# One multiplication of the second attention unit moved from VectorE to GpSimd, and the first stage's pieces put in another order

## The chip, the cores and the metric

The kernel runs on one core of a Trainium2 chip. A core has five engines that work side by side, each through its own list of instructions in order: TensorE (PE in the profile; its weight loads are listed apart as PEld), VectorE (DVE), ScalarE (ACT), GpSimd (POOL) and SyncE (SP), which here only starts DMA transfers. They share the on-chip memory SBUF, and TensorE writes its products into PSUM, a small memory of banks from which VectorE and ScalarE read. An engine waits for another on semaphores. The metric is the device time of one execution in microseconds; a time below is the median of several runs.

## The reference: what is computed

Two blocks in a row, all in float32. The first is a linear recurrent attention (RWKV-6) over batch 4, 8 heads, 768 steps, head width 48; the second a token and channel mixer.

```python
for t in range(S):                                   # S = 768
    cur = einsum('bhd,bhe->bhde', u * k_t, v_t)      # the step's own product, weighted by u
    y_t = einsum('bhd,bhde->bhe', r_t, state + cur)
    state = w_t[..., None] * state + einsum('bhd,bhe->bhde', k_t, v_t)
x = y.transpose(0, 2, 1, 3).reshape(B, S, 384)
u = x + (relu(x.T @ w_tok1) @ w_tok2).T              # 768 -> 256 -> 768 over the tokens
out = u + relu(u @ w_ch1) @ w_ch2                    # 384 -> 1536 -> 384 over the channels
```

## The kernel before, in words

The attention is cut into chunks of 64 steps, so that most of it becomes matrix products. A *unit* is a third of a batch (256 steps, which is four chunks, and 8 heads in four pairs): units 0, 1 and 2 are batch 0, and there are twelve in all. For each unit the code makes a set of *pieces*, small functions with names, and a table or a planner decides in which order the pieces are issued. The pieces of a unit `i`, by the names of the table:

- `i.ends` (VectorE): running products of w from a chunk's end backwards (a scan, L446), and a reciprocal (L447). `i.begins` (VectorE): running products from the beginning (a scan in place over w, L454).
- `i.own0` to `i.own3` (ScalarE, L342): k times u, a pair of heads each, into one buffer that all units share. `i.own` (TensorE, L326): products of that with r. `i.put` (VectorE, L469): its diagonal into the attention matrix `at`.
- `i.keys` (VectorE, L451): k scaled in place by the products of `ends`. `i.queries` (VectorE, L457): r scaled in place by those of `begins`; it needs `begins`, the loaded r, and the end of `i.own`, which reads r unscaled.
- `i.tokens` (TensorE, L356): the scaled k turned, into two PSUM banks; `i.copied0`, `i.copied1` (ScalarE, L361) copy them out. `i.gram` (TensorE, L326): scaled k with scaled r; `i.mask` (VectorE, L338) picks its lower part into `at`.
- `i.carry` (TensorE, L376): each chunk's contribution to the state, in PSUM. `i.by0` to `i.by3` (ScalarE, L512) scale the state into SBUF and `i.up0` to `i.up3` (TensorE, L519) add it to the next chunk's: a chain in which ScalarE and TensorE take turns. `i.by0` of the next unit goes on from the last `up` of this one.
- `i.before` (TensorE, L391): r with the states; `i.seen` (ScalarE, L400) reads one column of it; `i.after` (TensorE, L412) adds `at` times v; `i.taken0` to `i.taken2` (ScalarE, L418) copy the result into x.

Beside these run the conversions of the mixer's weights, which come from DRAM as 64-bit words: `t0` to `t2` for the token weights and `c0` to `c2` for the first of the channel weights. Each has a `load` (a DMA), `plus` (L275) and `minus` (L278) on ScalarE, and `lead` (L281), `two` (L284), `value` (L288) and `sum` (L292) on VectorE. Then the first mixing of batch 0 begins: `h0` to `h11` (TensorE, L958) are x times the token weights, an even number for the first 128 hidden columns and an odd one for the second, one pair for each 128 tokens; `relu0` (ScalarE, L961) rectifies the even sum and `relu1` the odd one, and `back0` (TensorE, L969) multiplies with the second token weights, first the part of `relu0`, then that of `relu1`.

Everything of units 0, 1 and 2 and of `t`, all of `c0` but its `sum`, the loads of `c1` and `c2`, the `h`s and `back0` is the *first stage*. Its order is written out by hand as a table, `FIRST`. Each name is a piece; `a<b` is a DMA that may only be issued once piece `b` has been. `strict()` makes the instructions of TensorE, VectorE, ScalarE and SyncE follow each other on their engine in the order of the table; GpSimd is not in that list, so its instructions stand in the order in which the code made them and wait for their data alone. The rest of the kernel is issued from a second table, `ORDER`, of almost 1,200 characters that says from which of nine streams the next piece comes.

GpSimd sets up masks at the start and from 187 us on adds up a part of the hidden layer's forms (L776); in the first stage it has nothing to do after the masks.

Of the kernel before, what the change touches and what calls it, by code (L numbers as in the profile page):

```python
# [23 lines left out]
T = 64  # L24
# [24 lines left out]
LEAST, MOST = 2.0 ** -40, 2.0 ** 40  # L49
MID = 3 * G // 4 * SEG1  # L50
FIRST = (
# [8 lines left out]
)  # L60
ORDER = (
    "8880080880788088000008884844408008408040a80a88080880a484408848840a0a4480884080088880a80080884808884040488844488888084840"
# [13 lines left out]
def rwkv6_then_mixer(  # L76
# [16 lines left out]
    pe, dve, act, pool, sp = nc.tensor, nc.vector, nc.scalar, nc.gpsimd, nc.sync  # L93
# [92 lines left out]
    def w_of(i):  # L186
        return ws[i if i < UB else 1]
# [232 lines left out]
    def unit(i):  # L420
# [3 lines left out]
        w_, at = w_of(i), ats[i % 2 if i < UB else 0]  # L424
        by_chunk = [t[:ROWS].rearrange("p (g t) -> p g t", t=T) for t in (r_, k_)]
        L = {"before": {}}

        def of_chunks(t, first, n):
            return t[:ROWS, :G * SEG1].rearrange("p (g s) -> p g s", s=SEG1)[:, :, first:first + n]
# [24 lines left out]
            dve.tensor_tensor_scan(w_[:ROWS], w_[:ROWS], starts[:ROWS], 0.0, op0=ALU.mult, op1=ALU.add)  # L454

        def queries():
            dve.tensor_mul(by_chunk[0], by_chunk[0], of_chunks(w_, 0, T))  # L457

        def own_u(a):
            if a == 0:  # L460
# [83 lines left out]
        def each(f, n):  # L544
            return [lambda m=m: f(m) for m in range(n)]

        return dict(small=lambda: ranges(0), large=lambda: ranges(1), ends=ends, keys=keys, begins=begins, queries=queries, own_u=each(own_u, A),
                    own_gram=own_gram, copied=each(copied, UC), taken=each(taken, 3),
                    own_put=own_put, products=[lambda n=n: products(n) for n in range(3)], sums_put=sums_put,
# [804 lines left out]
```

## Time and profile before

| what | value |
|---|---|
| time, median of 3 runs | 477.82 us (477.06 to 478.12) |
| the profiled execution's own time | 476.31 us |
| its span, first to last instruction | 474.6 us |
| PE, DVE, ACT, POOL busy | 459.4, 344.8, 265.4, 54.1 us |
| granted TensorE clock, mean | 0.999 |
| end of the first stage (`back0` begins) | 48.79 us |

The profile's times are microseconds from the start of the span. A row of the timeline reads: start, duration, engine, line of the program, operation, written tile<-read tile with partitions x elements, how many instructions were merged, and in brackets the idle time of the engine ahead of it with what released it. A matrix product of float32 leaves two records in the trace, so 32 products show as x64. Line numbers of the trace are those of the kernel before; in the changed kernel each stands one line lower.

### The profile page before, as it was taken

The page shows a single profiled execution, that of the slowest core. Times are in us where ns is not written, and L with a number is a line of the kernel's source. Part 1 is how long each engine was busy: PE and PEld are TensorE (multiplying, and loading weights), DVE is VectorE, ACT ScalarE, POOL GpSimd, SP SyncE. Part 2 cuts the span into 40 slices and gives each one's busy share as a digit, 9 for nine tenths or more (in the row PEclk, how much of TensorE's full clock was granted, in tenths as well). Part 3 has the DMA queues.
Part 4 walks back from the last instruction along what each step waited for, and adds up shares of the span by engine and source line. Part 5 has one row for each costly group of instructions (what it writes and reads, how often), then busy time and mean ns, then how long its engine had stood idle before and what let it go on. Part 6 is the DMA issues. An engine that isn't in the chain of part 4 may idle for free.

```text
span 474.6 us, 12781 instructions
## 1 busy us (share of the span) xinstructions
PE 459.4 (97%) x5322; PEld 410.8 (87%) x5322; DVE 344.8 (73%) x495; ACT 265.4 (56%) x606; POOL 54.1 (11%) x58
## 2 busy tenths in 40 slices
PE   3999999999999999999999999999999999999996
PEld 2876688856797668999999999999999999999995
DVE  7988896779598877876897998685587885235341
ACT  5588788774678856353747485351827554034140
POOL 1000000000000001230303002130304003032130
PEclk9999999999999999999999999999999999999999
DMA  8955944573585456953888841754775612436231
GB/s 301 338 185 197 296 162 146 191 266 99 157 224 146 171 183 209 281 188 99 257 276 251 286 157 51 213 168 130 228 223 141 186 48 84 122 96 201 85 99 54
DMA packets 45055, 85.34 MB, mean 180 GB/s; under 512 B 4736, under 2 KB 37376, under 8 KB 44992
## 3 DMA queue, kind: packets, MB, share of 16 engines
q1 hardware_dynamic: 44704, 84.37, 56.1%
q8 instruction: 43, 0.70, 0.6%
q14 instruction: 20, 0.16, 0.1%
q10 hardware_dynamic: 288, 0.10, 0.1%
HBM read 72.65 MB, written 11.80 MB: 178 GB/s over the span
## 4 chain that ended last, share of the span: by engine, by line
PE 96%; DMA 1%; ACT 1%; SPq 0%; issue 0%; DVE 0%; DVEq 0%
PE bank L1015 10%; PE bank L783 8%; PE bank L790 8%; PE bank L785 8%; PE bank L801 8%; PE bank L803 8%; PE bank L802 8%; PE bank L1004 7%; PE bank L678 3%; PE bank L1000 3%; PE bank L737 3%; PE bank L326 2%; PE bank L391 2%; PE kv_ps L376 2%; PE bank L412 2%; PE h_ps L958 2%
## 5 line engine op out<-in xcount | busy, mean ns | idle before, releaser
L776 POOL TENSOR_TENSOR z_high<-z_high 128x384 fp32r<-128x384 f32 x48 | 52.9, 1106 | 405.0 <-DMA ring<-third 185.8
L765 ACT ACTIVATE z_high<-bank 128x384 fp32r<-128x384 f32 x48 | 23.5, 489 | 57.4 <-PE bank L790 56.9
L783 PE MATMUL bank<-x_forms,forms 128*128 128x384 f32 x216 | 50.3, 340 | 0.0
L790 PE MATMUL bank<-z_more,forms 128*128 128x384 f32 x216 | 50.1, 340 | 0.0
L785 PE MATMUL bank<-x_forms,ring 128*128 128x384 f32 x216 | 49.3, 337 | 0.0
L772 DVE SCALAR_TENSOR_TENSOR z_high<-bank,z_high 128x384 fp32r<-128x384 f32 x48 | 26.6, 555 | 31.4 <-ACT z_high L765 29.3
L1015 PE MATMUL bank<-wch,z 128*128 128x384 f32 x144 | 48.1, 488 | 0.0
L801 PE MATMUL bank<-forms,z_high 128*128 128x384 f32 x140 | 47.8, 342 | 0.0
L803 PE MATMUL bank<-forms,z_high 128*128 128x384 f32 x140 | 47.2, 337 | 0.0
L802 PE MATMUL bank<-ring,z_high 128*128 128x384 f32 x140 | 47.1, 337 | 0.0
L809 DVE SCALAR_TENSOR_TENSOR x<-bank,x 128x384 f32<-128x384 f32 x35 | 18.8, 553 | 38.9 <-PE bank L803 38.7
L1015 PEld LDWEIGHTS bank<-wch,z 128*128 128x128 f32 x144 | 26.8, 190 | 17.2
L512 ACT ACTIVATE before<-state,to_end 112x48 f32<-112x48 f32 x132 | 33.2, 324 | 13.0 <-DVE state L527 7.6
L790 PEld LDWEIGHTS bank<-z_more,forms 128*128 128x128 f32 x216 | 39.0, 188 | 0.1
L783 PEld LDWEIGHTS bank<-x_forms,forms 128*128 128x128 f32 x216 | 38.3, 188 | 0.5
L785 PEld LDWEIGHTS bank<-x_forms,ring 128*128 128x128 f32 x216 | 38.6, 188 | 0.0
L1004 PE MATMUL bank<-xT,wch 128*128 128x256 f32 x144 | 32.0, 381 | 0.0
L1004 PEld LDWEIGHTS bank<-xT,wch 128*128 128x128 f32 x144 | 27.0, 190 | 3.7
L768 ACT ACTIVATE z_high<-z_high 128x384 fp32r<-128x384 f32 x48 | 25.2, 525 | 3.6
L801 PEld LDWEIGHTS bank<-forms,z_high 128*128 128x128 f32 x140 | 26.3, 188 | 0.2
L802 PEld LDWEIGHTS bank<-ring,z_high 128*128 128x128 f32 x140 | 26.3, 188 | 0.0
L803 PEld LDWEIGHTS bank<-forms,z_high 128*128 128x128 f32 x140 | 26.3, 188 | 0.0
(250 smaller groups left out, 963.6 us busy)
## 6 DMA issues: line engine op xcount, KB each, us to landing
ring<-third SPq DMA_DIRECT2D x144, 192.0 KB, 3.3
raw<-in_words_ch_dram SPq DMA_DIRECT2D x8, 1023.8 KB, 4.9
rk<-in_rk_dram SPq DMA_DIRECT2D x36, 192.0 KB, 5.2
near<-in_near_dram SPq DMA_DIRECT2D x8, 768.0 KB, 4.9
w<-in_w_dram SPq DMA_DIRECT2D x10, 520.5 KB, 5.0
vt<-in_v_dram SPq DMA_DIRECT2D x12, 384.0 KB, 5.1
out_dram<-x SPq DMA_DIRECT2D x17, 192.0 KB, 2.1
third<-forms SPq DMA_DIRECT2D x12, 192.0 KB, 4.2
```

The lines of the kernel that those rows point to most:

```text
L512: act.mul(t[:ROWS, a], state[bt, g][:ROWS, a], by_last(c, j)[:, a:a + 1])
L768: act.mul(z_form(jt, 2), z_form(jt, 0).bitcast(f32), 1.0 / BASE)
L772: dve.scalar_tensor_tensor(z_form(jt, 1), a, 0.0, z_form(jt, 0).bitcast(f32), op0=ALU.max, op1=ALU.subtract)
L776: pool.tensor_add(z_form(jt, 2), z_form(jt, 2).bitcast(f32), z_form(jt, 1).bitcast(f32))
L783: pe.matmul(a, up[m], xf(0)[:, m], start=m == 0, stop=False)
L785: pe.matmul(a, low[:, m], xf(1)[:, m], start=False, stop=False)
L790: pe.matmul(banks["a", jt], joint, xf(2)[:, m], start=False, stop=m == 2)
L801: pe.matmul(a, z[0], up, start=first, stop=False, skip_group_check=True)
L802: pe.matmul(a, z[1], held[bt, s, half, 1, jt], start=False, stop=False, skip_group_check=True)
L803: pe.matmul(a, z[2], joint, start=False, stop=last, skip_group_check=True)
L1004: pe.matmul(ps, now["wch1"][:, jt // 4, m, ts(jt % 4, 128)], xT[:, m, ts(s, SEG)], start=(m == 0), stop=(m == DM // 128 - 1))
L1015: pe.matmul(ps, zs[s][:, jt, ts(n, 128)], now["wch2"][:, jt, :], start=(jt == 0), stop=(jt == NJ - 1))
```

## The change

`queries` of unit 1 is issued on GpSimd in place of VectorE; the operation and its operands are the same. And the table `FIRST` is replaced by another order of the same pieces: no piece is added or left out. Of the table's lines the last ones are shown.

```diff
 FIRST = (
...
-    "2.taken1 t2.value 2.taken2 h7 h8 c0.plus h10 t2.sum c0.minus c2.load<1.tokens c0.lead c0.two relu0 h9 h11 relu1 rk3 c0.value back0 "
+    "h7 h6 h9 h11 c1.load<2.own w3<2.by3 rk3 c0.minus h8 t2.value t2.sum c0.plus h10 relu1 c0.lead c2.load<1.tokens c0.two relu0 c0.value "
+    "back0 v3"
 )
...
         def queries():
-            dve.tensor_mul(by_chunk[0], by_chunk[0], of_chunks(w_, 0, T))
+            (pool if i == 1 else dve).tensor_mul(by_chunk[0], by_chunk[0], of_chunks(w_, 0, T))
```

Three places show what moves. VectorE first, in the stretch around the scaled r of unit 1. The tiles: `rk_89` is r and k of unit 1, `w_90` its w, `x` holds the w of unit 2 for now, and `first` on the left of a product is k of unit 2 or the second `at`. Before:

```order
L469 TENSOR_TENSOR first<-gram,u_rows 128x1024
L338 COPY_PREDICATED at_92<-before_it,gram 128x1024
L442 MEMSET starts 112x17
L446 SCALAR_TENSOR_TENSOR ahead<-x,starts 112x1041
L447 RECIPROCAL starts<-ahead 112x16
L457 TENSOR_TENSOR rk_89<-rk_89,w_90 112x1024
L451 TENSOR_TENSOR first<-first,ahead 112x1024
L281 TENSOR_TENSOR raw<-raw 128x1024
```

and in the changed kernel:

```order
L455 SCALAR_TENSOR_TENSOR w_90<-w_90,starts 112x1041
L339 COPY_PREDICATED at_92<-before_it,gram 128x1024
L443 MEMSET starts 112x17
L447 SCALAR_TENSOR_TENSOR ahead<-x,starts 112x1041
L448 RECIPROCAL starts<-ahead 112x16
L455 SCALAR_TENSOR_TENSOR x<-x,starts 112x1041
L470 TENSOR_TENSOR first<-gram,u_rows 128x1024
L452 TENSOR_TENSOR first<-first,ahead 112x1024
L282 TENSOR_TENSOR raw<-raw 128x1024
```

`1.queries` is gone from VectorE, `2.begins` (the scan over `x`) has come forward to stand right behind `2.ends`, and `1.put` stands behind both scans.

The second place is ScalarE between the end of unit 0 and the chain `by`/`up` of unit 1 (`before<-kv_ps,ahead` is a `by`). Before:

```order
L512 ACTIVATE before<-kv_ps,ahead 112x48 x4
L418 COPY x<-y_ps 128x8x48
L278 ACTIVATE raw<-raw,rebias 128x1024
L418 COPY x<-y_ps 64x8x48
L512 ACTIVATE before<-kv_ps,ahead 112x48 x4
L418 COPY x<-y_ps 64x8x48
L512 ACTIVATE before<-kv_ps,ahead 112x48 x4
```

and in the changed kernel:

```order
L513 ACTIVATE before<-kv_ps,ahead 112x48 x4
L343 ACTIVATE near<-first,u_col 112x2x128 x2
L419 COPY x<-y_ps 128x8x48
L343 ACTIVATE near<-first,u_col 112x2x128
L419 COPY x<-y_ps 64x8x48
L343 ACTIVATE near<-first,u_col 112x2x128
L513 ACTIVATE before<-kv_ps,ahead 112x48 x4
L279 ACTIVATE raw<-raw,rebias 128x1024
L513 ACTIVATE before<-kv_ps,ahead 112x48 x4
```

Between `1.by0` and `1.by1` the conversion step of 1,024 columns has given way to the four steps of `2.own`; a conversion step now stands between `1.by1` and `1.by2`.

The third is TensorE from `1.gram` on. Its list is the same up to there, piece by piece. Before:

```order
L326 MATMUL gram<-rk_89 64x64 x32
L519 MATMUL kv_ps<-before,ident 112x192
L391 MATMUL y_ps<-before,rk_89 64x48 x32
L376 MATMUL kv_ps<-vt,kT 48x48 x24
L519 MATMUL kv_ps<-before,ident 112x192
L958 MATMUL h_ps<-x,wtok_125 128x384 x2
L519 MATMUL kv_ps<-before,ident 112x192
L958 MATMUL h_ps<-x,wtok_125 128x384
L412 MATMUL y_ps<-vt,first 64x48 x32
```

and in the changed kernel:

```order
L327 MATMUL gram<-rk_89 64x64 x32
L392 MATMUL y_ps<-before,rk_89 64x48 x32
L520 MATMUL kv_ps<-before,ident 112x192
L959 MATMUL h_ps<-x,wtok_125 128x384 x2
L377 MATMUL kv_ps<-vt,kT 48x48 x24
L520 MATMUL kv_ps<-before,ident 112x192
L413 MATMUL y_ps<-vt,first 64x48 x32
L520 MATMUL kv_ps<-before,ident 112x192
L959 MATMUL h_ps<-x,wtok_125 128x384 x2
```

The `h`s stand in two pairs where there were a pair and single ones; seven `h`s end the stage in both kernels, even ones first before (`h8 h10`, then `h9 h11`) and odd ones first now (`h9 h11`, then `h8 h10`).

On SyncE's queue the load of unit 1's w stands two transfers earlier, `c1.load` stands ahead of the loads for unit 3, and the load of unit 3's v comes last.

14 rows, old and new, of the table FIRST are left out of this document.

## The prediction

> **What bounds the kernel now.** I read first the page's list of busy times, then the table by stage, then the timeline of the first 50 us, where everything lies that the change touches.
>
> ```profile
> span 474.6 us, 12781 instructions
> PE 459.4 (97%) x5322; PEld 410.8 (87%) x5322; DVE 344.8 (73%) x495; ACT 265.4 (56%) x606; POOL 54.1 (11%) x58
> ```
> ```profile
> 140.00:300.00 160.00, 159.72 (x1978) 143.15 (x1978) 131.19 (x192) 96.46 (x226) 22.59 (x20) 1.00 0.63 195
> ...
> 25.90:44.17 18.27, 17.52 (x601) 13.46 (x596) 15.23 (x17) 15.58 (x43) 0.00 (x0) 1.00 0.52 173
> 44.17:50.45 6.28, 6.28 (x26) 3.60 (x20) 5.31 (x7) 5.62 (x8) 0.00 (x0) 1.00 1.02 401
> ```
>
> Columns: stretch, length, then busy time of PE, PEld, DVE, ACT, POOL. TensorE sets the time. Between 140 and 300 us it stands still for 0.28 us of 160, so what the first stage saves or loses is passed on to the end almost whole. And the first stage itself is held by TensorE: from 25.9 us to the run of `h`s it is idle for 18.27 - 17.52 = 0.75 us, and from there to the end of `back0` for nothing. A new order of the same pieces can therefore win 0.75 us there and what single products waste, and no more.
>
> Where those 0.75 us lie, from the timeline of TensorE and ScalarE:
>
> ```profile
> 25.90 1.21 PE L376 MATMUL kv_ps<-vt,kT 64*48 64x48 f32 x64
> 27.04 0.58 PE L519 MATMUL kv_ps<-before,ident 112*112 112x192 f32 x2
> 27.55 1.16 PE L326 MATMUL gram<-first,near 48*64 48x64 f32 x64
> 29.23 0.58 PE L519 MATMUL kv_ps<-before,ident 112*112 112x192 f32 x2 [0.52 <-ACT before L512]
> ...
> 30.77 0.58 PE L519 MATMUL kv_ps<-before,ident 112*112 112x192 f32 x2 [0.20 <-ACT before L512]
> ...
> 40.23 0.91 PE L958 MATMUL h_ps<-x,wtok 128*128 128x384 f32 x2
> ...
> 44.17 4.78 PE L958 MATMUL h_ps<-x,wtok 128*128 128x384 f32 x14
> ```
> ```profile
> 26.19 0.48 ACT L418 COPY x<-y_ps 128x384 f32<-128x384 f32 x1 [1.03 <-PE y_ps L412]
> 26.56 1.22 ACT L278 ACTIVATE raw<-raw,rebias 128x1024 int16<-128x1024 int16 x1
> 27.81 0.48 ACT L418 COPY x<-y_ps 64x384 f32<-64x384 f32 x1
> 28.30 0.88 ACT L512 ACTIVATE before<-kv_ps,ahead 112x48 f32<-112x48 f32 x4
> ```
>
> `1.up1` at 29.23 and `1.up2` at 30.77 wait for ScalarE, 0.52 and 0.20 us, not for VectorE. `1.by1` could have begun when `1.up0` ended, at 27.62; it began at 28.30 since the conversion step of 1.22 us stood ahead of it. No wait of TensorE here is on the multiplication that moves.
>
> **The multiplication on GpSimd.** What it removes and what stands in its place:
>
> ```profile
> 10.32 1.23 DVE L457 TENSOR_TENSOR rk<-rk,first 112x1024 f32<-112x1024 f32 x1 [0.24 <-PE gram L326]
> ...
> 15.46 2.31 DVE L454 TENSOR_TENSOR_SCAN w<-w,starts 112x1041 f32<-112x1041 f32 x1
> ...
> 17.69 1.20 DVE L451 TENSOR_TENSOR rk<-rk,ahead 112x1024 f32<-112x1024 f32 x1
> ...
> 19.11 1.22 DVE L469 TENSOR_TENSOR first<-gram,u_rows 128x1024 f32<-128x1024 f32 x1 [0.22 <-PE gram L326]
> ...
> 20.25 1.30 DVE L338 COPY_PREDICATED at<-before_it,gram 128x1024 f32<-128x1024 uint8 x1
> ...
> 21.61 2.33 DVE L446 TENSOR_TENSOR_SCAN ahead<-x,starts 112x1041 f32<-112x1041 f32 x1
> 23.98 0.26 DVE L447 RECIPROCAL starts<-ahead 112x16 f32<-112x16 f32 x1
> 24.15 1.16 DVE L457 TENSOR_TENSOR rk<-rk,w 112x1024 f32<-112x1024 f32 x1
> ...
> 27.82 0.69 DVE L281 TENSOR_TENSOR raw<-raw 128x1024 int16<-128x1024 int16 x1 [1.38 <-ACT raw L278]
> ...
> 31.27 1.23 DVE L292 TENSOR_TENSOR wtok<-wtok,raw 128x1024 f32<-128x1024 f32 x1
> ```
> ```profile
> 17.05 1.99 PE L326 MATMUL gram<-rk,near 48*64 48x64 f32 x64
> ```
> ```profile
> 187.72 1.02 POOL L776 TENSOR_TENSOR z_high<-z_high 128x384 fp32r<-128x384 f32 x1 [185.75 <-DMA ring<-third]
> ```
>
> VectorE loses one instruction of 1.16 us. GpSimd has done no product of 1,024 columns in this trace. Its addition of 384 columns takes 1.02 us alone; by width that is 1.02 x 1024/384 = 2.72 us, the upper bound for it undisturbed. If a part of it does not grow with the width, it is less: VectorE's 0.94 us for 768 columns (212.89, below) and 1.16 for 1,024 leave 0.28 us that are fixed, and with as much fixed on GpSimd it is 0.28 + 0.74 x 1024/384 = 2.25 us, the lower bound. I take 2.7, the nearer row being GpSimd's own. It can begin when `1.begins` and `1.own` are done. The list of TensorE up to `1.own` is unchanged, which puts that end at 19.04 (17.05 + 1.99); VectorE, walked with its rows (`0.queries` to 11.55, then a `put` of 1.22, a scan of 2.33, a reciprocal of 0.26, `keys` of 1.20 and a scan of 2.31), comes to 18.9. So GpSimd multiplies from 19.1 to 21.8. The result is needed by `1.gram`, at 31.28 before, ten microseconds later: its own duration costs nothing, even doubled.
>
> What it disturbs is another matter, since while GpSimd runs, VectorE may not:
>
> ```profile
> 209.25 1.33 DVE L484 COPY_PREDICATED at<-diagonal,sums 128x1024 f32<-128x1024 uint8 x1
> 210.47 1.76 DVE L724 TENSOR_TENSOR spare<-spare 128x768 fp32r<-128x768 f32 x1
> ...
> 212.89 0.94 DVE L724 TENSOR_TENSOR spare<-h_room,spare 128x768 fp32r<-128x768 f32 x1
> ```
> ```profile
> 209.50 1.92 POOL L776 TENSOR_TENSOR z_high<-z_high 128x384 fp32r<-128x384 f32 x1 [0.55 <-DVE z_high L772]
> 212.87 1.83 POOL L776 TENSOR_TENSOR z_high<-z_high 128x384 fp32r<-128x384 f32 x1 [1.45 <-DVE z_high L772]
> ```
> ```profile
> 190.27 1.28 DVE L499 TENSOR_TENSOR at<-bank,strictly 128x512 f32<-128x512 f32 x2
> 190.50 1.02 POOL L776 TENSOR_TENSOR z_high<-z_high 128x384 fp32r<-128x384 f32 x1 [0.28 <-DVE z_high L772]
> ```
>
> GpSimd's 1.02 us became 1.92 beside a VectorE instruction that reads two SBUF tensors, and the subtraction behind it took 1.76 in place of 0.94, up to GpSimd's end and then its own length. Beside an instruction that reads PSUM and SBUF (190.27) nothing grew. They take turns, whole instructions at a time. The Trainium skill, GPSIMD Engine Reference, section 8 (Key points), says that GpSimd shares its SBUF interfaces with VectorE and contends with instructions of two SBUF inputs there; the trace agrees, 1.76 against 0.94 us. Its section 4.1 (Engine selection) advises VectorE for such a product, GpSimd being about twice as slow; an estimate by that is 2.3 us, inside my bounds.
>
> In the new order VectorE has `0.mask` next to `1.begins` (18.9 to 20.2, products from PSUM, so no turn is due), then the scan of `2.ends`, with two SBUF inputs. No scan meets GpSimd in this trace; between no wait and a wait to GpSimd's end I take the wait, by the row of 1.76. The scan runs from 21.8 to 24.1, `2.begins` to 26.6, `1.put` to 27.7. A stall of 1.6 us for an instruction of 1.16 saved. What is late next: `2.keys`. But that has to wait for ScalarE's four steps of `2.own` in any case,
>
> ```profile
> 20.74 1.31 ACT L342 ACTIVATE near<-first,u_col 112x256 f32<-112x256 f32 x3
> ```
>
> which the new list puts among the copies of unit 0's result (26.19 before). From that copy on there are two of these steps of 1.31/3 = 0.44 and two copies of 0.4 each: they end at 27.7 to 27.9. So the stall is just covered; `2.keys` runs to 29.0, in time for `2.tokens` (29.64 before), and `t0.sum`, which with `2.put` took VectorE from 27.82 to 32.50, 4.7 us, reaches 33.7, when the first `h` is due at 33.9. Cost 0, with a margin of 0.2 us. Without the cover it would be 1.6 us.
>
> **The new order, step by step.**
> 1. `1.by1` has only short steps ahead of it now, so it begins at 27.7 and `1.up1` follows `2.own` at 28.7: **-0.5**.
> 2. `t1.minus`, 1.22 us, now stands between `1.by1` and `1.by2`: that ends at 30.5, `1.up2` begins at 30.55 in place of 30.77. Of the 0.5 won, 0.2 are left: **+0.3**.
> 3. `h`s: a single one took 0.91 us, while in the run of 14 records each takes 4.78/7 = 0.68. One single has become part of a pair: **-0.2**.
> 4. `2.carry` now comes behind `1.up3` and two `h`s and needs `2.by0`, which ScalarE does behind `t1.plus` (about 32.9 to 34.1): done at 35.0, when the pair of `h`s ends too: **+0.1** for the hand-over.
> 5. The end. Before, `relu0` ran while TensorE did `h9 h11`:
>
> ```profile
> 48.05 0.48 ACT L961 ACTIVATE h<-h_ps 128x384 f32<-128x384 f32 x1
> ...
> 48.79 1.66 PE L969 MATMUL kv_ps<-h,wtok 128*128 128x384 f32 x4
> ...
> 48.99 0.49 ACT L961 ACTIVATE h<-h_ps 128x384 f32<-128x384 f32 x1 [0.46 <-PE h_ps L958]
> ...
> 49.53 0.30 PEld L969 LDWEIGHTS kv_ps<-h,wtok 128*128 128x128 f32 x2 [0.55 <-ACT h L961]
> ```
>
> `back0` began with `relu0`'s half at once and met `relu1` half-way; from the last `h` (48.95) to the end of `back0` (50.45) it was 1.5 us, with TensorE never idle. Now `h8 h10` come last, so `relu0` is the last thing that `back0`'s first product waits for: 0.48 us and two hand-overs of some 0.06, idle, then 1.3 us of products: 1.9 to 2.0. **+0.5**.
>
> The sum is -0.5 + 0.3 - 0.2 + 0.1 + 0.5 = **+0.2 us**. The loads cost nothing: unit 1's k comes behind its w now, but ahead of unit 0's v, so no later than that w was there before, and `1.own0` is not due before the first copy of k is out, at about 12; the loads behind it keep their distance to their use. The profiled execution took 476.31 us; with the change 476.5. It lies 1.51 under the median of the runs shown, so on their scale 477.82 + 0.2 = **478.0 us**. What can be told from no change here is about 0.2%, 0.96 us.
>
> **Rivals.**
> - *GpSimd waits for its turn and the scan waits for GpSimd* (slower). The mechanism above, one step on: if `0.mask`, which reads its mask from SBUF, counts like the `COPY_PREDICATED` at 209.25, GpSimd begins at 20.2 and ends at 22.9. The scan follows, `2.keys` ends at 30.0, `t0.sum` at 34.7, and the first `h` is 0.8 late with all of TensorE's list behind it: +1.0 in sum, 478.8; if the two take turns more than once, another 0.5, 479.3. It decides from a GpSimd end of about 22.0 on. For it: the rows at 209 us, and a margin of 0.2. Against: the mask instruction here reads its data from PSUM. A chance of 0.23.
> - *The order packs* (faster). All 0.75 us of idle time go, and two singles instead of one (0.45); `relu0` costs its 0.5 only in part, because ScalarE is free earlier there and TensorE's last products end sooner. Then -1.0 to -1.2, 476.7. For it: all waits are on ScalarE, which is freed of a conversion step ahead of `1.by1`. Against: the end of the stage, which no slack on ScalarE can mend, since `relu0` needs `h10`. 0.17.
> - *The move does nothing, the order all*: with `1.queries` left on VectorE, 1.16 us of work there but without the stall of 1.6, `2.keys` would still wait for ScalarE. Time as forecast; it is part of the forecast's chance.
>
> **How the numbers follow.** Forecast 0.60, port 0.23, packing 0.17. The forecast's own range is 477.2 to 478.8. Taking in both other cases and a spread of the medians as the runs show it (477.06 to 478.12), 8 in 10 lie between 476.8 and 479.2. Faster by over 0.2% (under 476.9): most of packing, 0.16. Slower (over 478.8): port, and the upper edge of the forecast, 0.24. The same: 0.60.
>
> **What would show it.** In the changed profile: GpSimd's product at 19 us with 2.2 to 2.8 us if undisturbed (over 3.4 says that it waited for a turn); the scan of `2.ends` beginning at GpSimd's end, or lasting longer, not at 20.2; `1.up1` without a wait, `1.up2` with one of about 0.5; TensorE idle by 0.5 ahead of `back0`, which begins at 49.5 where it began at 48.79. I am wrong if the first `h` waits for `t0.sum`, or if the time after 50 us changes by more than what the first stage hands on.

## The result, and the profile after

The changed kernel takes 478.92 us (median of 12 executions, 477.15 to 482.57), the kernel before 476.80 beside it (12 executions, 474.01 to 478.12). The ratio is 1.0056, with a 95% interval of 1.003 to 1.0081: slower by 0.56%, some 2.7 us, where 0.2 us was forecast. The ratios here and below leave out executions over 1.5% above the fastest of the same kernel (three of twelve and one of six in the last two kernels, one of the kernel before); the medians are of all.

Executions of one kernel scatter more here than the difference between the two kernels, and a profile shows only one of them. Six of the twelve of the changed kernel took 477.15 to 478.33 us and six 479.51 to 482.57; the profiled one, 479.51 us, is of the second six, so what it waits for need not hold for the first.

The tables by stage of both kernels, first the changed one (columns: stretch, length, busy time of PE, PEld, DVE, ACT, POOL, then the granted clock of TensorE, the DMA share and GB/s):

```profile
10.00:26.00 16.00, 12.10 (x392) 10.24 (x392) 15.83 (x14) 11.70 (x34) 2.18 (x1) 1.00 0.90 316
26.00:34.00 8.00, 6.12 (x184) 5.39 (x187) 7.80 (x9) 5.94 (x17) 0.00 (x0) 0.79 0.48 152
34.00:54.00 20.00, 18.52 (x376) 12.38 (x369) 12.69 (x17) 14.21 (x32) 0.00 (x0) 1.00 0.75 241
54.00:140.00 86.00, 86.00 (x790) 65.87 (x789) 69.48 (x89) 62.16 (x125) 0.00 (x0) 1.00 0.55 177
```

and the kernel before:

```profile
10.00:26.00 16.00, 15.00 (x345) 12.93 (x341) 15.18 (x15) 9.55 (x30) 0.00 (x0) 1.00 0.83 305
26.00:34.00 8.00, 7.28 (x282) 6.07 (x280) 6.54 (x8) 6.92 (x23) 0.00 (x0) 1.00 0.62 198
34.00:54.00 20.00, 19.97 (x356) 13.08 (x353) 17.05 (x21) 16.07 (x31) 0.00 (x0) 1.00 0.72 247
```

Nearly all of it is lost in the first stage: `back0` begins at 51.68 instead of 48.79, 2.89 us later, and the span is 3.2 us longer (477.8 against 474.6). Between 10 and 26 us TensorE is even ahead, with 392 records done against 345. Then it does 184 in eight microseconds where it did 282, idle for 1.9 us and at a granted clock of 0.79, and between 34 and 54 us it is idle for another 1.5 us. TensorE no longer holds the stage; it waits. What for, from its timeline:

```profile
10.38 1.73 PE L357 MATMUL k_ps<-ident,rk 112*128 112x112 f32 x8 [0.62 <-issue]
...
23.39 0.94 PE L377 MATMUL kv_ps<-vt,kT 64*48 64x48 f32 x64 [0.77 <-ACT before L513]
...
27.00 1.16 PE L327 MATMUL gram<-first,near 48*64 48x64 f32 x64 [2.17 <-ACT before L513]
28.09 0.94 PE L520 MATMUL kv_ps<-before,ident 112*112 112x192 f32 x2
...
30.32 0.85 PE L520 MATMUL kv_ps<-before,ident 112*112 112x192 f32 x2
31.09 1.36 PE L327 MATMUL gram<-rk 48*64 48x64 f32 x64
...
33.44 1.07 PE L392 MATMUL y_ps<-before,rk 48*64 48x48 f32 x57 [0.88 <-issue]
...
38.95 1.01 PE L413 MATMUL y_ps<-vt,first 64*64 64x48 f32 x51 [0.90 <-issue]
...
46.16 4.94 PE L959 MATMUL h_ps<-x,wtok 128*128 128x384 f32 x14
51.68 1.56 PE L970 MATMUL kv_ps<-h,wtok 128*128 128x384 f32 x4 [0.58 <-ACT h L962]
```

The row of `1.gram` (31.09) stands in the kernel before as

```profile
31.28 1.16 PE L326 MATMUL gram<-rk 48*64 48x64 f32 x64
```

TensorE's list is the same in both kernels up to `1.gram`, so up to there nothing is lost on balance: it comes there 0.19 us earlier, having gained by fast products what it lost by the waits of 0.77 and 2.17 us. What is lost comes behind. From `1.gram` to `back0` the changed kernel takes 20.59 us, the one before 17.51, 3.08 more; 0.88 and 0.90 of these are the two waits for "issue" and 0.58 is the wait ahead of `back0`.

VectorE and GpSimd beside it:

```profile
18.46 1.28 DVE L339 COPY_PREDICATED at<-before_it,gram 128x1024 f32<-128x1024 uint8 x1
...
19.81 3.32 DVE L447 TENSOR_TENSOR_SCAN ahead<-x,starts 112x1041 f32<-112x1041 f32 x1
...
23.46 2.33 DVE L455 TENSOR_TENSOR_SCAN x<-x,starts 112x1041 f32<-112x1041 f32 x1
25.70 1.20 DVE L470 TENSOR_TENSOR first<-gram,u_rows 128x1024 f32<-128x1024 f32 x1
```
```profile
18.77 2.18 POOL L458 TENSOR_TENSOR rk<-rk,w 112x1024 f32<-112x1024 f32 x1 [16.81 <-DVE w L455]
```

The wait of 2.17 us at `2.own` (27.00) is put down to ScalarE's `1.by1`, which `2.own` does not read and which ended at 26.71; what ended at 26.90 is `1.put` (25.70 + 1.20), which reads the tile that `2.own` writes; in a run below the same wait is put down to `1.put` by name. `1.put` stands behind both scans of unit 2 now, and the first of them took 3.32 us instead of 2.33 because GpSimd was multiplying. The wait of 0.58 us ahead of `back0` is the one for `relu0`. Three waits, 2.4 us together, are for "issue": time in which TensorE waited for nothing that the profile shows. The kernel before has none in this stage.

### The profile page after: what moved, and what is told of

Read it like the earlier page. It is cut to its first block, busy times and chain, and to the rows that moved or that the text cites. A ratio compares the mean times of both kernels' runs of the same rounds, so it can differ in the third digit from the quotient of the medians.

```text
span 477.8 us, 12782 instructions
## 1 busy us (share of the span) xinstructions
PE 457.2 (96%) x5322; PEld 408.8 (86%) x5322; DVE 344.2 (72%) x494; ACT 265.1 (55%) x606; POOL 56.7 (12%) x59
## 4 chain that ended last, share of the span: by engine, by line
PE 94%; ACT 2%; issue 1%; DMA 1%; SPq 0%; DVE 0%; DVEq 0%; ACTq 0%
PE bank L1016 10%; PE bank L784 8%; PE bank L791 8%; PE bank L786 8%; PE bank L802 8%; PE bank L804 8%; PE bank L803 8%; PE bank L1005 7%; PE bank L679 3%; PE bank L738 3%; PE bank L1001 3%; PE bank L327 2%; PE bank L413 2%; PE bank L392 2%; PE h_ps L959 2%; PE gram L327 2%
```

## The experiments

The kernels ran in five groups, each on one chip, beside executions of the kernel before on the same chip; a ratio is against those. The medians of the kernel before were 476.84, 476.60, 476.01, 476.76 and 476.60 us.

### The two parts of the change apart

One kernel has the order of before and the GpSimd product, the other the new order and all products on VectorE:

```diff
-            dve.tensor_mul(by_chunk[0], by_chunk[0], of_chunks(w_, 0, T))
+            (pool if i == 1 else dve).tensor_mul(by_chunk[0], by_chunk[0], of_chunks(w_, 0, T))
```


> The order of before, with the scaling of r of unit 1 on GpSimd: the move alone. Theory P (the loss comes of 1.put standing behind two scans, the first of which waits for GpSimd, so that TensorE waits for it): here 1.put and 0.mask read PSUM and stand ahead of the scan of 2.ends, so GpSimd (from 19.0 to 21.2 in a cold run) is done before the scan begins and nothing is late. Time as before, within 1 us. Theory G (a GpSimd instruction costs by itself, by the port or otherwise, wherever it stands): slower by 1 us or more, with the scan lengthened or TensorE waiting behind it.

> The new order with that multiplication back on VectorE: the order alone. Theory P: the scan of 2.ends loses its wait of 1.0 us, 1.put ends 1.0 us earlier, and 2.own waits about 1.2 us where it waited 2.2; still 1 to 2 us slower than before, about 1 us faster than the changed kernel. Theory G: as fast as before, since no GpSimd instruction is left. Theory R (the turned ends of h and relu are the loss): slower than before by 0.5 us alone.

The move alone: 477.29 us, ratio 1.0006 (0.9984 to 1.0028). The order alone: 480.29 us, 1.0069 (1.0042 to 1.0096). The move costs nothing that can be measured, and the order alone is as slow as both. With the order alone the scan lasts 2.33 us, as before, so the loss does not need GpSimd's turn at the memory.

### The two waits mended, one at a time and together

`1.put` ahead of the scans; the even `h`s and `relu0` ahead of the odd ones; both:

```diff
-... 0.by3 0.mask 2.ends 1.tokens 1.copied1 1.copied0 0.before t0.minus 2.begins 1.put 0.up3 ...
+... 0.by3 0.mask 1.put 2.ends 1.tokens 1.copied1 1.copied0 0.before t0.minus 2.begins 0.up3 ...
```
```diff
-h7 h6 h9 h11 c1.load<2.own w3<2.by3 rk3 c0.minus h8 t2.value t2.sum c0.plus h10 relu1 c0.lead c2.load<1.tokens c0.two relu0 ...
+h7 h6 h8 h10 c1.load<2.own w3<2.by3 rk3 c0.minus h9 t2.value t2.sum c0.plus h11 relu0 c0.lead c2.load<1.tokens c0.two relu1 ...
```


> The changed kernel with 1.put moved on VectorE from behind the two scans to ahead of 2.ends, where it runs while GpSimd does. Theory P: 2.own no longer waits (2.2 us less idle), TensorE's clock does not fall again at 28 us, and the time comes down by 2 to 3 us, to that of before or below. If the loss lies in the other idle times (0.9 us twice of its own sequencer, 0.6 ahead of the last stage): at most 0.5 us less than the changed kernel.

> The changed kernel with the two ends of the first mixing exchanged back: h8 h10 ahead of h9 h11, and relu0 ahead of relu1. Theory R: the wait of 0.58 us ahead of back0 goes, and the time with it: 0.5 us less than the changed kernel, 2 us over before. If 2.own's wait and the clock are the loss, the same 0.5 us and no more.

> The changed kernel with both repairs: 1.put ahead of the scan of 2.ends, and the even sum first at the end. Theory C: executions with a clock that rises late at 476.5 to 477.5, those with an early one still slower, since the waits of ScalarE's chain by and up are left; median 477 to 478. If 1.put's wait and the end were the whole loss: 476 or below.

`1.put` early: 479.94 us, 1.007 (1.004 to 1.01). It mends nothing. Even ones first: 479.17, 1.0044 (1.0009 to 1.0079), a part of it at best, within the intervals. Both: 479.52, 1.0054 (1.0029 to 1.008). So taking away these two waits, singly or together, does not bring the time back, and the theory that `1.put` behind the scans is the loss fell. In the profile with both mended (481.86 us) the waits for "issue" have taken the room:

```profile
24.70 0.56 PE L327 MATMUL gram<-first,near 48*64 48x64 f32 x20
27.67 0.92 PE L327 MATMUL gram<-first,near 48*64 48x64 f32 x44 [2.40 <-issue]
...
37.32 0.43 PE L413 MATMUL y_ps<-vt,first 64*64 64x48 f32 x13
39.20 1.73 PE L413 MATMUL y_ps<-vt,first 64*64 64x48 f32 x51 [1.45 <-issue]
```

A group of equal products breaks off in its middle, after 20 records of 64, and goes on 2.40 us later. The second wait begins after 13 of 64, at the same place as the wait of 0.90 us in the changed kernel, which stands ahead of 51 as well.

### Sixteen products more, ahead of the first stage and behind it

TensorE's clock was the next suspect. In the profile before its products run at half pace until 25.8 us, in the one after they are fast from 16.6 us on. Products ahead of the first stage should bring the fast clock early in every kernel:

```diff
+    def dummies(n):
+        for _ in range(n):
+            pe.matmul(warm[:, :128], ident, ident, start=True, stop=True)
+
+    strict(lambda: dummies(16))
     for name in FIRST.split():
```


> The order of before, with 16 extra products of 128x128 by 128 ahead of the first stage, while TensorE waits for its first data; they write a bank that nobody reads. Theory C (what decides is when TensorE's clock rises in the first stage, and whether it falls again when TensorE has run ahead and waits): the clock is up from 8.3 us in nearly every execution. The old order has its pieces ready early, so it gains: the end of the first stage by walked rows 2.8 us sooner if the clock stays up, time 474 to 475.5. Theory O (the new order is longer whatever the clock): the same gain of 2 to 3 us, which alone tells nothing; it is told apart by the next run.

> The changed kernel with the same 16 products ahead. Theory C: with a high clock TensorE comes to 2.own 2 to 3 us before 1.put is done, waits there, and the clock falls again: no gain or a loss, 479 to 482 in nearly all executions, none at 477; 4 us or more over the old order with the same products. Theory O: a gain of 2 to 3 us as in the old order, 476 to 477.

> Both repairs and the 16 products ahead. Theory C: better than the changed kernel with the products alone by 2 us or more, since 2.own no longer waits for 1.put (walked rows: first stage 1.8 us shorter than before's if the clock never fell, so 475); if the clock falls all the same, 478 to 481, and then it is not 1.put alone that lets it fall.

> The kernel before with 16 more products of 128x128x128 behind the last piece of the first stage instead of ahead of the first (they cost some 1.0 us there by the 0.06 us of one at the full clock; their sums are not read). If the longer instruction stream is what cost 8 us with the products at the start: 482 to 485, with waits for instructions in the later stages. If it was the early clock of the first stage: 477 to 478.5.

All of them lost: the kernel before with them takes 484.8 us, 1.0182 (1.0149 to 1.0214); the changed one 486.7, 1.0203 (1.0166 to 1.024); the one with both waits mended 485.61, 1.0195 (1.0161 to 1.0229). With the sixteen products at the end of the stage, where they cannot touch its clock, the kernel before takes 487.95, 1.0195 (1.0153 to 1.0238). There they cost 3.73 us themselves, not the 1.0 that I had put. Part of the rest shows in the waits of TensorE, most of them behind both the products and the stage; at the start:

```profile
PE bank L412 <- issue: 2.8, 2, 2.5
PE kv_ps L376 <- issue: 2.5, 2, 1.8
PE bank L801 <- issue: 1.3, 1, 1.3
...
PE bank L1015 <- issue: 1.0, 1, 1.0
```

and at the end of the stage:

```profile
PE bank L412 <- issue: 3.1, 1, 3.1
...
PE bank L1015 <- issue: 1.1, 1, 1.1
PE bank L801 <- issue: 0.4, 1, 0.4
```

5.1 and 4.6 us of these lie after 54 us, on the same three lines, in stages that nobody had changed. So the times of these kernels say nothing on the early clock. The profile of the kernel before with the products shows that it came: the first 64 records took 1.24 us from 8.06 on, not 1.99; yet `back0` began at 49.39 us, not earlier than the 48.79 without them. They say that a TensorE list that is 16 products longer makes TensorE wait for its own instructions far from where the 16 stand, at either place.

### The order cut at two places

TensorE's list is the same in both orders up to `1.gram`. The order of before and the new one were joined at `0.up0` (about 16 us) and at `1.gram` (about 28 us), the GpSimd product kept:

```diff
-FIRST = the new order
+FIRST = one order up to the cut, then the pieces that are left, in the sequence of the other
```


> The order of before up to and with 0.up0 (about the first 16 us), then what is left in the order of the change; the GpSimd product is kept. The new order loses about 2 us somewhere, and this and the next three runs cut it at two places. If the loss sits in the start (masks late, w1 and 0.copied1 early, 0.own before 1.own), this one is near before, 476.5 to 477.3. If it sits in the middle (1.put behind 2.ends, 2.own0-3 and 2.own ahead of 1.by1) or in the tail (2.before ahead of the masks of the third unit, relu0 last), it stays at 478.5 to 479.5.

> The complement: the order of the change up to 0.up0, then that of before. If the start carries the loss, 478.5 to 479.5; if the middle or the tail does, 476.5 to 477.3.

> The order of before up to and with 1.gram (about 28 us), then what is left in the order of the change. If only the tail costs (the relu that back0 waits for, 0.5 to 0.6 us by the run that swapped the state's pieces), 477.2 to 477.6. If the tail carries the whole loss (the small products of the third unit closer together, waits for instructions with them), 478.5 or more. If the start or the middle carries it beside the relu, not over 477.6.

> The complement: the order of the change up to 1.gram, then that of before. If the loss is all in the tail, 476.5 to 477.2. If the start and the middle carry what is beside the relu, about 478.3 to 479; more than 479 would mean that the two orders' ends do not add up and the loss hangs on the clock's course and not on a place.

| start | middle | tail | us | ratio, interval |
|---|---|---|---|---|
| before | new | new | 479.90 | 1.0080 (1.0053 to 1.0106) |
| new | before | before | 476.17 | 1.0006 (0.9985 to 1.0027) |
| before | before | new | 477.92 | 1.0037 (1.0009 to 1.0064) |
| new | new | before | 478.71 | 1.0059 (1.0035 to 1.0082) |

The start costs nothing that can be measured. Middle and tail cost something each; their sum, 0.96%, lies above the 0.56% of the whole change, but the intervals do not separate the two.

### Which engine in the middle, what in the tail

From the kernel with the tail of before (478.71 us) one engine's sequence was put back, every other engine's unchanged; and the tail alone got its even `h`s and `relu0` first. VectorE's sequence:

```diff
-1.ends 1.keys ... 1.begins ... 0.mask 2.ends 1.tokens ... 2.begins 1.put 0.up3 ...
+1.ends ... 1.begins ... 1.keys ... 1.put 1.tokens 0.mask 2.ends ... 0.up3 ... 2.up0 h1 h0 2.begins ...
```

ScalarE's:

```diff
-... 1.copied1 1.copied0 0.before t0.minus ... 0.seen ... t0.plus 1.by0 ... 2.own0 2.own1 0.taken0 ... 2.own2 0.taken1 2.own3 ...
+... 2.own0 2.own1 ... 2.own2 0.before 1.copied0 t0.plus 0.seen ... 2.own3 1.copied1 1.by0 ... 0.taken0 1.carry t0.minus ...
```


> Start and middle in the order of the change, tail as before (478.7 us in that form), but VectorE's sequence is that of before throughout: 1.put ahead of 0.mask and 2.ends, 2.begins in the tail. No other engine's sequence moves. If VectorE's order in the middle (the 2.33 us of 2.begins and the scan drawn out by GpSimd, both ahead of 1.put) is the loss: 476.2 to 477.0. If ScalarE's is: 478.2 to 479.2. If the two share it: 477.3 to 478.

> The same kernel, but with ScalarE's sequence of before in the middle (2.own0-3 ahead of 1.by0, t0.minus and t1.minus later) and VectorE's of the change. If ScalarE's order is the loss (the four 2.own conversions at 25.5 to 28.1 us and two word conversions ahead of 1.by0, for which TensorE's 1.carry and 2.own wait .74 and .47): 476.2 to 477.0. If VectorE's is: 478.2 to 479.2. If they share it: 477.3 to 478.

> Start and middle as before, tail in the order of the change (477.92, +1.9 us over before in its call), but with h8 and h10 ahead of h9 and h11 and relu0 ahead of relu1, so that back0 waits for no relu. If the relu is the tail's whole cost: 476 to 476.6. If it is its 0.58 us alone, the rest being the wait of 1.36 us for the words of t0.sum behind 2.begins: 477.2 to 477.6.

VectorE's put back: 476.31 us, 1.0002 (0.9979 to 1.0025); the whole 0.59% is gone. ScalarE's put back: 477.33, 1.0029 (1.0004 to 1.0054); half of it, a difference that the two intervals leave open. The tail with even ones first: 476.51, 0.9993 (0.9969 to 1.0017); all of the tail's 0.37%. In the run with ScalarE's old sequence VectorE's scan meets GpSimd in full, and TensorE waits for `1.put` by name:

```profile
19.89 3.97 DVE L446 TENSOR_TENSOR_SCAN ahead<-x,starts 112x1041 f32<-112x1041 f32 x1
...
26.43 1.20 DVE L469 TENSOR_TENSOR first<-gram,u_rows 128x1024 f32<-128x1024 f32 x1
```
```profile
27.69 1.16 PE L326 MATMUL gram<-first,near 48*64 48x64 f32 x64 [0.76 <-DVE first L469]
```

With VectorE's sequence of before the scan takes 2.33 us again and starts behind GpSimd:

```profile
21.21 2.33 DVE L446 TENSOR_TENSOR_SCAN ahead<-x,starts 112x1041 f32<-112x1041 f32 x1
```

### The two findings put together

If VectorE's middle and the relu are the loss, the new order with both mended is as fast as the kernel before. The first kernel moves `2.begins` behind `1.mask`, with even ones first, the second moves `1.put` ahead of `2.ends` as well:

```diff
-... 0.before t0.minus 2.begins 1.put 0.up3 ... 2.copied1 1.mask h1 h3 ...
+... 0.before t0.minus 1.put 0.up3 ... 2.copied1 1.mask 2.begins h1 h3 ...
```


> The change with the state's pieces in even order (479.17 in that form) and, of VectorE's sequence alone, 2.begins moved from ahead of 1.put to behind 1.mask. 1.put stays behind 2.ends. If 2.begins at its early place is the loss: 476.2 to 477.2. If 1.put's place counts as well, though it mended nothing by itself: 477.3 to 478.3. If it is neither but the clock's course in all kernels with this order: 478.6 to 479.6.

> The same with 1.put ahead of 2.ends as well, which leaves the start, ScalarE's middle, the tail and the GpSimd product of the change. By the two kernels that put back VectorE's sequence (476.31) and the relu order (476.51) one at a time: 475.8 to 476.8, as before or up to 0.2% below. If ScalarE's middle and the new tail cost something together that neither costs alone: 477.3 or more.

It is not: 479.53 us, 1.0057 (1.0029 to 1.0084), and 482.01, 1.0104 (1.0052 to 1.0156). Each part put back was the whole of its loss while the other part of the order was as before; these two kernels, with both mended, are no faster than the change. But they do not put back all of VectorE's sequence: `1.keys` still stands ahead of `1.begins`, and `0.mask` ahead of `1.put`. VectorE's whole old sequence with the new tail, even ones first, has not been run, so that what is left of VectorE's order is not ruled out as the cause. Their profiled executions took 484.20 and 487.30 us, well above the medians, and wait 6.4 and 8.4 us for "issue" in the first stage; these sums are of those executions and not of the median.

### What the waits for "issue" are

Beside the loads, the trace shows single packets of 16 KB on a DMA queue of the kind "instruction". Eighteen waits for "issue" in the first stage, in six profiles (the changed kernel 2, both waits mended 3, the tail of before 1, VectorE's put back 1, the last two kernels 6 and 5), end 1.26 to 1.50 us after such a packet has landed. They stand at fixed places of TensorE's list, seventeen of them ahead of records 477, 604, 730, 857 and 985 (within one), so a packet holds what makes some 127 records. (The waits of 0.2 to 0.8 us at about 10.4 us, behind the first 64 records, come before any such packet; what they wait for is not seen.) In the changed kernel the third packet landed at 25.74 us and the next began only at 31.21. SyncE's queue says what is between:

```profile
26.74 0.33 SPq L273 DMA_DIRECT2D xT<-in_words_tok_dram  x1
32.53 0.33 SPq L273 DMA_DIRECT2D z<-in_words_ch_dram  x1
36.53 0.33 SPq L273 DMA_DIRECT2D raw<-in_words_ch_dram  x1
```

`t2.load`, 1 MB, is issued at 26.74. The DMA view from 27.70 to 31.20 us holds its packets,

```profile
q1 hardware_dynamic: 143, 1.05, 84.3%
```

and from 31.20 to 32.20 the instruction packet, as soon as they are through:

```profile
q8 instruction: 1, 0.02, 5.8%
q1 hardware_dynamic: 1, 0.00, 0.1%
```

TensorE resumes at 33.44, 1.30 us after its landing at 32.14. The next two packets begin at 36.74 and 40.71, where the packets of the next two loads come to their end (36.9 and 41.1); TensorE waits for the first of them (0.90 us) and not for the second. In the kernel before, `t2.load` is issued at 29.20, `c0.load` at 32.51 and `c1.load` at 42.67:

```profile
29.20 0.33 SPq L272 DMA_DIRECT2D xT<-in_words_tok_dram  x1
32.51 0.33 SPq L272 DMA_DIRECT2D z<-in_words_ch_dram  x1
...
42.67 0.88 SPq L272 DMA_DIRECT2D raw<-in_words_ch_dram  x2
```

There the fourth packet begins at 29.10, ahead of the load's packets, and the one at 41.24 finds no load under way; the one between, at 33.52, also begins only as the packets of `t2.load` end, and is in time all the same. The reading is that an instruction packet queues behind a load whose packets are already under way, and that in such executions of the new order loads of 1 MB get ahead of packets that TensorE needs soon.

The other profiles bear it out for `t2.load`. Of the sixteen without the sixteen products, four have a wait at record 604 (changed, both waits mended, and the last two kernels), and in these four the fourth packet begins within 0.25 us of the end of that load's packets (31.21, 30.84, 30.89 and 33.55 us). In the twelve others it begins before them, or in one 0.24 us after the first of them, and TensorE does not wait there. It is a near thing: with VectorE's sequence put back TensorE begins `1.up1` at 27.86 us, the packet begins at 28.10 and the load's packets at 28.23; in the changed kernel, where `1.put` held TensorE, `1.up1` begins at 28.09, and the load's packets have run since 27.70. That would tie VectorE's sequence to the waits. It is read from the times of single executions, and no run has tried it: a kernel with the new order and these loads held back would.

Take the waits for "issue" from a profiled execution's time, and the kernels without the sixteen products come closer together, from 475.8 to 487.3 us to 473.8 to 478.6 (one execution of each):

| kernel | profiled, us | "issue", us | rest, us |
|---|---|---|---|
| before | 476.31 | 0 | 476.3 |
| product alone | 477.50 | 0.3 | 477.2 |
| order alone | 478.07 | 1.1 | 477.0 |
| changed | 479.51 | 2.4 | 477.1 |
| `1.put` early | 478.35 | 0.5 | 477.9 |
| even ones first | 477.02 | 0.2 | 476.8 |
| both of these | 481.86 | 5.8 | 476.1 |
| start of before | 477.85 | 0.8 | 477.1 |
| only the start new | 476.85 | 0.3 | 476.5 |
| only the tail new | 478.09 | 0 | 478.1 |
| tail of before | 478.82 | 1.7 | 477.1 |
| VectorE's put back | 475.76 | 2.0 | 473.8 |
| ScalarE's put back | 476.60 | 1.2 | 475.4 |
| new tail, even first | 476.25 | 0.3 | 475.9 |
| `2.begins` late | 484.20 | 7.3 | 476.9 |
| `2.begins` late, `1.put` early | 487.30 | 8.7 | 478.6 |

The rest lies within 1 us of 477 in eleven of sixteen rows. The five with odd ones first in the new tail (order alone, changed, `1.put` early, start of before, only the tail new) are the five that wait 0.58 us for `relu0`, and have a mean rest of 477.4, the eleven others 476.4.

## Why the prediction was wrong, point by point

- **The multiplication on GpSimd, cost 0: right.** Alone it costs 0.0006 of the time, with an interval that holds zero. It took 2.18 us undisturbed, not the 2.7 that I took and below my lower bound of 2.25: by its own two rows, 1.02 us for 384 columns and 2.18 for 1,024, its fixed part is an estimated 0.32 us, where I lent it VectorE's 0.28. The Trainium skill, GPSIMD Engine Reference, section 4.1 (Engine selection), has GpSimd about twice as slow, which gave an estimate of 2.3; the trace, 2.18 against 1.16, agrees better with that than with my row by width.
- **The turns of GpSimd and VectorE: the mechanism right, its place in time off, its price not seen.** The scan was drawn out to 3.32 us in the changed kernel and to 3.97 beside ScalarE's old sequence. I let it begin at 21.8, behind GpSimd; it begins at 19.81, beside GpSimd, and ends 2.18 us after GpSimd does (20.95). In four profiles with VectorE's old sequence (the product alone among them) it is GpSimd that waits, for `1.keys`, and takes 2.67 to 2.82 us. The margin that I named was ScalarE's, ahead of `2.keys`. What was late was `1.put`, which `2.own` waits for: 2.17 us in one profile, 0.76 in another. I had let `1.put` end at 27.7, with TensorE at `2.own` no earlier than that.
- **"The loads cost nothing": the failed step.** The sum put the loads at nothing, by the use that is made of their data, and had no term at all for TensorE's own instructions. Its only measure of a load was its distance to its use; what else has to pass while `t2.load`, issued 2.5 us earlier, and `c1.load`, 6 us earlier, are under way was not asked. In the changed profile two waits for "issue", 0.88 and 0.90 us, stand behind `1.gram`, 1.78 of the 2.89 us by which `back0` is late. Each ends 1.3 us after an instruction packet has landed that began as a load's packets came to their end. That is the largest part in the profile. Whether it is the loss of the medians as well stays open: the one profile of the order alone (478.07 us, its median 480.29) has no such wait between 11 and 54 us.
- **Steps 1 and 2, -0.5 and +0.3: the number met, the way not; luck.** `1.up1` follows `2.own` without a wait, as forecast, at 28.09 (forecast 28.7); `1.up2` begins at 30.32 (forecast 30.55), without the wait of 0.5 that I named as a sign; `1.gram` is 0.19 us ahead, where the sum had 0.2. But I walked the list with the durations of one execution, in which products were slow until 25.8 us. In the changed profile they are fast from 16.6 us, and TensorE lost what that gained by waiting 0.77 us ahead of `1.carry` and 2.17 ahead of `2.own`, with a granted clock of 0.79 over the eight microseconds from 26 on. In the profile with even ones first, where products are slow as before, `1.gram` is 0.51 us late (31.79), `1.up2` waits 0.54 us, and `back0` begins at 48.79, as before.
- **The first `h` and `t0.sum`.** In the changed kernel the first `h` (34.85) does not wait, so this sign of being wrong did not come. With the tail alone it waits 1.36 us for `t0.sum`, and 1.08 in the tail with even ones first, which is as fast as before.
- **Step 5, `relu0` last, +0.5: right, 0.58** in the profiles of all five kernels that end so, without the sixteen products. In the tail alone, turning the ends back takes away the whole 0.37%, some 1.8 us, more than the wait itself; what the rest is, is not shown.
- **Rivals.** "Port" forecast 478.8, near what came, but for another reason: the order alone, without the product, is as slow. "Packing" did not happen. "The move does nothing, the order all" is what the runs say of the parts, and I had counted it to the forecast, with its time: the order was the loss.
- **The range** of 476.8 to 479.2 holds 478.92, but on the scale of three runs whose median was 477.82. With the forecast put on 476.80, the median of the executions beside it, the range would be 475.8 to 478.2, and the change lies above it; that the range as stated holds it is luck.

What is settled: the product and the start of the new order cost nothing that can be measured; the order is the loss; in the middle it goes with VectorE's sequence, at the end with the even ones first, as long as the other part is as before. What stays open is why the two together, mended in part, still lose 0.6 to 1.0%, and so the cause of the whole loss. That instruction packets queue behind loads fits the times of sixteen profiles, and is not shown by a run.

## What to carry to other kernels

An order worked out from one profile is only as good as that execution's pace: ask of each gain what an engine that comes sooner will wait for next, and read the waits for "issue" as a resource of their own, which a load under way may hold up. Mend a new order by putting back one engine's sequence at a time, with the others unchanged, but try the mends together, and whole, before believing their sum. A filler product is no neutral probe: sixteen of them cost the kernel before 8.2 and 11.2 us here, 5.1 and 4.6 of it in waits for instructions behind the first stage.

## What was not expected of the hardware

- By the times of the traces TensorE's instructions arrive in packets of 16 KB, each for some 127 records of small products, and a late one costs up to 2.4 us at once in these profiles. In the kernel before, the third packet lands at 26.29 us and TensorE reaches that place 1.6 us later, hardly more than the 1.26 to 1.50 us that the late ones take from landing to use; it was tight there already.
- The moment at which TensorE's products become fast differs from one execution to the next: 16.6 us in the changed kernel and about 26.6 in the one with even ones first, whose lists are the same up to the tail. The granted clock stands at 1.00 in the profile's rows from 10 to 26 us in both the kernel before (fast from 25.8) and the changed one. Early speed is no gain by itself. The kernel in which only the start is new shows the clock at 0.50 from 20 to 28 us after having been fast, and takes 476.17 us, like the kernel before.
- GpSimd and VectorE took turns at SBUF by whole instructions here too: a scan of 2.33 us became 3.32 and 3.97, ending 2.18 us after GpSimd did in both, while the mask beside it (1.28 us against 1.30) did not change.
